# Windowed attention with a maxout feed-forward layer: a rewritten opening, masks added by TensorE, and Q in runs of four tokens

## The chip, the cores and the metric

The kernel runs on one core of a Trainium2 chip. The metric is the time of the program on the device in microseconds (us); a time given for a kernel is the median of several runs. A profile is one execution taken by the hardware profiler. Engines: PE is TensorE (matmul; PEld its weight loads), DVE is VectorE, ACT is ScalarE, POOL is GpSimd, SP is SyncE, which here only issues transfers. Each engine takes its instructions in the order of the program.

## What is computed

Four batches, eight heads, 768 tokens, head size 64. A query sees the first four tokens (the sink) and the 128 tokens up to itself. The result of attention, with the heads side by side, goes through a feed-forward layer that takes the maximum of three products.

```python
def _attn_ref(q, k, v, n_sink, window):            # n_sink 4, window 128
    scores = scale * np.matmul(q, k.transpose(0, 1, 3, 2))
    rel = pos[:, None] - pos[None, :]
    keep = (pos[None, :] < n_sink) | ((rel >= 0) & (rel < window))
    scores = np.where(keep, scores, -1000000000.0)
...
    return np.matmul(softmax(scores), v)           # softmax in words of numpy

x = attn_out.transpose(0, 2, 1, 3).reshape(B * S, H * D)     # 3072 x 512
h = np.maximum(np.maximum(x @ w1, x @ w2), x @ w3)           # 3072 x 768
return h @ w_out                                             # 3072 x 512, float32
```

## The kernel before

**Chunks.** The work is cut into 12 chunks of 256 tokens (three per batch; c is the chunk's place in its batch, and c = 0 has no chunk before it). A chunk has four pairs of heads p, each with two heads a. Each chunk goes through these steps, and all engines' orders are written out by hand; the framework adds the semaphores.

- `load` (L67): K, Q and V of the chunk, 0.5 MB each in float32, one transfer each on SP's queue. A partition holds a run of two tokens (i), 512 bytes, for each head. Two raw buffers per tensor.
- `cast` (L340, `cast_qk` L86, `cast_v` L95): to bf16, on POOL in the loop.
- `turn` (L100) or `turn_dma` (L113): K and Q are turned so that the head's 64 dimensions lie on partitions. `turn` uses eight PE transposes per tensor and copies (DVE for K, ACT for Q). `turn_dma` issues two transposing transfers of 64 partitions per tensor on SP (L117).
- `score` (L199): per pair two PSUM banks `st`, in which up to four blocks of 128 keys by 128 queries lie side by side (two half windows for each of two query halves). `sink_score` (L225): the four sink keys of all pairs in one bank, for c > 0.
- `expo` (L218): exp on ACT per head (L222), then one product with a 0/1 mask on DVE per pair (L223).
- `av_open`, `av` (L251, L266): values, with a column of ones that gives the sum; then reciprocal (L282) and product (L285) on DVE give `x_sb`.
- `xpose` (L290, PE and ACT) or `xpose_dma` (L299, one transposing transfer of 128 partitions on SP): x turned into `xT`.
- `ffn_h` (L307): eight matmuls for two of six blocks of the hidden layer and one of three weights; the first weight's result is copied by ACT (L320), the others are joined by a maximum on DVE (L322). Nine such groups per chunk.
- `ffn_y` (L326): six matmuls per half chunk, a copy by ACT (L333). `store` (L335): two transfers of 64 partitions on SP, since the queries lie in the order of Q's runs of two.

PSUM is one ring of eight banks (L55), so a matmul group waits until the group eight before it has been read.

**Opening (L350 to L433).** Chunk 0 goes through in two halves of its heads; POOL makes masks and the constants of the sink, then issues the weight transfers `load_w` (float32 to bf16, 0.75 MB written each) between its casts. Chunks 0, 1 and 2 are turned by PE, chunk 3 by SP.

**Loop (L435 to L476), i from 2.** A pass scores chunk n = i + 1, runs the hidden layer of chunk i and the output of chunk i - 1, and turns chunk i + 2. On SP its order is: loads of i + 3, turns of K and Q of i + 2, store of i - 1, turn of x of n.

Of the kernel before, what the change touches and what calls it, by code (L numbers as in the profile page):

```python
# [16 lines left out]
def kernel(  # L17
# [30 lines left out]

    with tc.manual_schedule():
# [7 lines left out]

        RING = 4
        kT = [const.tile([128, 2, NP, 2, 64], BF16, name=f"kT{i}") for i in range(RING)]
        qT = [const.tile([128, 2, NP, 2, 64], BF16, name=f"qT{i}") for i in range(RING)]  # L60
# [6 lines left out]
        def load(ci, what="kqv", eng=None, parts=1, gate=None):  # L67
            if ci >= NCH:
                return
            b, c = divmod(ci, CPB)  # L70
            t0 = c * 256
            for w in what:
                src = {"k": k, "q": q, "v": v}[w]
                if (ci, w) not in raws:
                    raws[ci, w] = raw.tile([128, H, 2, D], F32, tag=w + "_raw", name=w + "_raw")
                dst = raws[ci, w]
                if gate is not None:
                    gate.memset(dst[0:1, 0, 0, 0:1], 0.0)
                n = H // parts
                for g in range(parts):  # L80
                    (eng or nc.sync).dma_start(
                        out=dst[:, n * g:n * g + n],
                        in_=src[b, n * g:n * g + n, t0:t0 + 256]
                            .rearrange("h (p i) d -> p h (i d)", i=2))

        def cast_qk(ci, w, g, eng):  # L86

            if (ci, w) not in bfs:
                bfs[ci, w] = raw.tile([128, NP, 2, 2, D], BF16, tag=w + "_bf", name=w + "_bf")
            x, y = bfs[ci, w], raws[ci, w]  # L90
            eng.tensor_copy(  # L91
                x[:, 2 * g:2 * g + 2].rearrange("q p i a d -> q p a i d"),
                y[:, 4 * g:4 * g + 4].rearrange("q (p a) i d -> q p a i d", a=2))
# [6 lines left out]
        def turn(ci, w, g):  # L100

            pt = bank([128, 2, 2, 128], BF16, "pt")
            x = bfs[ci, w]
            for p in range(2):
                for i in range(2):
                    nc.tensor.transpose(  # L106
                        pt[:, p, i], x[:, 2 * g + p, i].rearrange("q a d -> q (a d)"), ident)
            dst = (kT if w == "k" else qT)[ci % RING]
            (nc.vector.tensor_copy if w == "k" else nc.scalar.copy)(
                dst[:, :, 2 * g:2 * g + 2].rearrange("q n p i r -> q n (p i) r"),  # L110
                pt.rearrange("q p i (n r) -> q n (p i) r", r=64))

        def turn_dma(ci, w):  # L113
            dst = (kT if w == "k" else qT)[ci % RING]
            x = bfs[ci, w].rearrange("q p i a d -> q (p i a d)")
            for n in range(2):
                nc.sync.dma_start_transpose(  # L117
                    out=dst[:, n].rearrange("q p i r -> q (p i) r"), in_=x[64 * n:64 * n + 64])

        load(0, "k", nc.sync, 2)  # L120
        load(0, "q", nc.scalar, 2)
        load(0, "v", nc.sync)
        load(1, "kqv", nc.sync)

        ident = const.tile([128, 128], BF16, name="ident")
        make_identity(nc, ident)
        sel = const.tile([128, 32], BF16, name="sel")


        msk = const.tile([128, 2, 4, 128], BF16, name="msk")  # L130
        msk0 = const.tile([128, 2, 3, 128], BF16, name="msk0")

        def masks():
            nc.gpsimd.memset(msk[:, 0, 0:2], 1.0)
            for i in range(2):
                hp = slice(64 * i, 64 * i + 64)
                nc.gpsimd.affine_select(
                    out=msk[hp, 0, 1], in_=msk[hp, 0, 1], compare_op=ALU.is_ge, fill=0.0,
                    base=-i, pattern=[[1, 2], [2, 64]], channel_multiplier=-2)
                nc.gpsimd.affine_select(  # L140
                    out=msk[hp, 0, 0], in_=msk[hp, 0, 0], compare_op=ALU.is_gt, fill=0.0,
                    base=i, pattern=[[-1, 2], [-2, 64]], channel_multiplier=2)
            nc.gpsimd.tensor_copy(msk0[:, 0, 0], msk[:, 0, 1])
            nc.gpsimd.tensor_copy(msk0[:, 0, 1], msk[:, 0, 0])
            nc.gpsimd.tensor_copy(msk0[:, 0, 2], msk[:, 0, 1])
            for i in range(2):
                nc.gpsimd.memset(msk0[64 * i:64 * i + 2, 0, 0:2], 1.0)
            nc.gpsimd.tensor_copy(msk0[:, 1], msk0[:, 0])

        def masks_late():  # L150
            nc.gpsimd.tensor_copy(msk[:, 0, 2:4], msk[:, 0, 0:2])
            nc.gpsimd.tensor_copy(msk[:, 1], msk[:, 0])

        bm = const.tile([128, 2], F32, name="bm")

        def sink_init():

            nc.gpsimd.memset(sel, 0.0)
            for a in range(2):
                nc.gpsimd.tensor_copy(  # L160
                    sel[:, 4 * a:4 * a + 4].rearrange("q (r i) -> q r i", i=2),
# [3 lines left out]

            nc.gpsimd.memset(bm, 0.0)
            for p in range(NP):
                nc.gpsimd.memset(bm[32 * p:32 * p + 8], 1.0)
                nc.gpsimd.affine_select(
                    out=bm[32 * p:32 * p + 8], in_=bm[32 * p:32 * p + 8], compare_op=ALU.is_ge,  # L170
                    fill=0.0, base=0, pattern=[[-4, 2]], channel_multiplier=1)
                nc.gpsimd.affine_select(
                    out=bm[32 * p:32 * p + 8], in_=bm[32 * p:32 * p + 8], compare_op=ALU.is_ge,
                    fill=0.0, base=3, pattern=[[4, 2]], channel_multiplier=-1)
# [9 lines left out]
        w_sb = []  # L184

        def load_w(wi):
            w = (moe_w1, moe_w2, moe_w3)[wi]
            wt = const.tile([128, DS, d_ff], BF16, name=f"w{wi}")
            nc.gpsimd.dma_start(out=wt, in_=w.rearrange("(a p) f -> p a f", p=128))
            w_sb.append(wt)  # L190
# [8 lines left out]
        def score(ci, pairs):  # L199
            b, c = divmod(ci, CPB)  # L200
            kc, qc = kT[ci % RING], qT[ci % RING]
            for p in pairs:
                st = [bank([128, 4, 128], F32, "st") for a in range(2)]
                for s, x, n, q0, q1 in ((0, kT[(ci - 1) % RING], 1, 0, 1), (1, kc, 0, 0, 2),
                                        (3, kc, 1, 1, 2)):
                    if s == 0 and c == 0:
                        continue
                    for a in range(2):
                        hp = slice(64 * a, 64 * a + 64)
                        nc.tensor.matmul(  # L210
                            st[a][:, s:s + q1 - q0],
                            lhsT=x[hp, n, p].rearrange("q i r -> q (i r)"),
                            rhs=qc[hp, q0:q1, p].rearrange("q n i r -> q n (i r)"),
                            start=True, stop=True)
# [3 lines left out]
        def expo(ci, p):  # L218
            lo = 0 if ci % CPB else 1
            e, st = es[ci, p]  # L220
            for a in range(2):
                nc.scalar.activation(e[:, a, lo:], st[a][:, lo:], AF.Exp, scale=scale)  # L222
            nc.vector.tensor_mul(e[:, :, lo:], e[:, :, lo:], msk0 if lo else msk)  # L223

        def sink_score(ci):  # L225
# [4 lines left out]
            for p in range(NP):  # L230
                nc.tensor.matmul(  # L231
                    st[32 * p:32 * p + 32], lhsT=ks[b % 2][:, p],
                    rhs=qT[ci % RING][:, :, p].rearrange("q n i r -> q n (i r)"),
                    start=True, stop=True, tile_position=(0, 32 * p))
            e = work.tile([128, 2, 128], BF16, tag="e_sink", bufs=2, name="e_sink")
            nc.scalar.activation(e, st, AF.Exp, scale=scale)  # L236
            es[ci, "sink"] = e

        def sink_v(b):
# [3 lines left out]
            for p in range(NP):  # L243
                nc.tensor.matmul(
                    sv[32 * p:32 * p + 32], lhsT=sel, rhs=x[:, 0, 2 * p:2 * p + 2],
                    start=True, stop=True, tile_position=(0, 32 * p))
            nc.vector.tensor_mul(vs[b % 2], sv, bm.unsqueeze(2).to_broadcast([128, 2, D + 1]))
# [87 lines left out]
        def store(ci, t0=0, t1=2):  # L335
            dst = out[ci * 256:ci * 256 + 256].rearrange("(t r i) d -> i r t d", t=2, i=2)
            for i in range(2):
                nc.sync.dma_start(out=dst[i, :, t0:t1], in_=ys[ci][64 * i:64 * i + 64, t0:t1])

        def cast(ci):  # L340
            if ci >= NCH:
                return
            for w in "kq":
                for g in range(2):
                    cast_qk(ci, w, g, nc.gpsimd)
# [4 lines left out]
        for x in vb:  # L350
            nc.vector.memset(x[:, :, :, D:D + 1], 1.0)
        masks()
        for g in range(2):
            for w in "kq":
                cast_qk(0, w, g, nc.vector)
                turn(0, w, g)
            score(0, range(2 * g, 2 * g + 2))
            for p in range(2 * g, 2 * g + 2):
                expo(0, p)
        for n in range(2):  # L360
            for i in range(2):
                cast_v(0, n, i, nc.gpsimd)
        load_w(0)
        load_w(1)
        sink_init()
        sink_k(0)
        masks_late()
        for g in range(2):
            cast_qk(1, "k", g, nc.vector)
            cast_qk(1, "q", g, nc.gpsimd)  # L370
        load_w(2)
        for n in range(2):
            for i in range(2):
                cast_v(1, n, i, nc.gpsimd)
        load_wo()
        av_open(0)
        for p in range(NP):
            av(0, p)
        xpose(0, 0)
        xpose(0, 1)  # L380
        for g in range(2):
            turn(1, "k", g)
            turn(1, "q", g)
        sink_v(0)
        sink_score(1)
        score(1, range(NP))
        expo(1, 0)
        expo(1, 1)
        load(2, gate=nc.vector)
        ffn_h(0, 0, 0)  # L390
        expo(1, 2)
        ffn_h(0, 1, 0)
        expo(1, 3)
# [124 lines left out]
```

## Time and profile before

| What | Value |
|---|---|
| Runs | 204.31, 205.11, 205.56 us; median 205.11 |
| Profiled execution | 206.73 us, span 205.0 us |
| PE matmuls of the hidden layer (L314) | 864, 107.1 us busy |
| exp (L222) | 96, 49.4 us busy; idle before 6.3 |
| mask product (L223) | 48, 34.2 us busy |
| maximum (L322) | 72, 49.2 us busy |
| casts on POOL (L91, L96) | 13.4 + 14.8 + 31.2 us busy |
| DMA queue of SP | 68992 packets, 31.73 MB |
| loads of K, Q, V | 0.5 MB each, 5.8, 6.6, 7.1 us from issue to landing |
| turn of K, Q, x by transfer | 4.4, 3.0, 3.3 us from issue to landing |
| weights | 7.2 us from issue to landing, `w_out` 9.1 |

The span runs from the first to the last instruction. A row of busy time is the sum over the instructions of one line. Matmuls are pipelined, so their busy time is longer than the spacing at which they are issued. A transfer's time is counted from its issue on the queue to the landing of its last byte. The granted clock is a share of TensorE's full speed.

### The profile page before, as it was taken

How to read it: one execution, taken by the hardware profiler on the slowest of the kernel's cores; microseconds unless marked ns; L12 is line 12 of the kernel's file. 1: busy time of each engine (PE TensorE's matmuls, PEld its weight loads, DVE VectorE, ACT ScalarE, POOL GpSimd, SP SyncE). 2: the span in 40 equal slices, each digit the busy share in tenths (PEclk: the TensorE clock that was granted, in tenths of full speed). 3: DMA queues.
4: the chain of work that ended last, by engine and by line, in shares of the span. 5: the costliest groups of instructions: out<-in, count | busy, mean ns of one | idle time of the engine just before them, and what ended most of it. 6: DMA issues, size and time to landing. Idle time of an engine off the chain costs nothing.

```text
span 205.0 us, 4504 instructions
## 1 busy us (share of the span) xinstructions
PE 174.1 (85%) x1788; PEld 129.8 (63%) x1800; DVE 111.5 (54%) x239; ACT 88.9 (43%) x177; POOL 71.9 (35%) x139
## 2 busy tenths in 40 slices
PE   0345978999739999999967999999999899999990
PEld 0223755896624976858735958858678488685860
DVE  1247263264831683864934845937739368286340
ACT  2412772225423537348163148264272661742321
POOL 7298702779204602611802706408227000000000
PEclk9999995799976999999997999999999999999999
DMA  5999999993569829979999989789899963142404
GB/s 153 290 200 204 184 161 290 294 276 105 132 109 299 167 52 252 176 176 295 96 137 294 181 218 243 165 207 244 146 268 167 173 110 99 35 102 51 106 0 102
DMA packets 72436, 35.68 MB, mean 174 GB/s; under 512 B 30176, under 2 KB 69344, under 8 KB 72416
## 3 DMA queue, kind: packets, MB, share of 16 engines
q1 hardware_dynamic: 68992, 31.73, 74.1%
q0 software_dynamic: 2368, 3.15, 9.9%
q10 hardware_dynamic: 1056, 0.52, 1.0%
q8 instruction: 14, 0.23, 0.5%
q14 instruction: 6, 0.05, 0.1%
HBM read 25.17 MB, written 6.29 MB: 153 GB/s over the span
## 4 chain that ended last, share of the span: by engine, by line
PE 48%; DMA 14%; ACT 11%; DVE 10%; issue 8%; SPq 4%; POOL 2%; DVEq 0%
PE h_ps L314 30%; PE y_ps L331 8%; ACT e_sb L222 7%; DMA xT<-x_sb 5%; DMA qT<-q_bf 4%; PE st L210 4%; DVE h_sb L322 3%; DMA q_raw<-in_q_dram 3%; DVE x_sb L285 3%; SPq L117 3%; PE pt L106 2%; PE o L277 2%; DMA k_raw<-in_k_dram 2%; ACT y_sb L333 2%; DVE e_sb L223 2%
## 5 line engine op out<-in xcount | busy, mean ns | idle before, releaser
L314 PE MATMUL h_ps<-xT,w 128*128 128x256 bf16 x864 | 107.1, 280 | 3.2 <-DMA xT<-x_sb 3.2
L314 PEld LDWEIGHTS <-w 128*128 128x128 bf16 x864 | 83.6, 100 | 17.4 <-DMA xT<-x_sb 5.0
L223 DVE TENSOR_TENSOR e_sb<-e_sb,msk 128x1024 bf16<-128x1024 bf16 (+1 forms) x48 | 34.2, 712 | 58.9 <-ACT e_sb L222 55.9
L322 DVE TENSOR_TENSOR h_sb<-h_sb,h_ps 128x512 bf16<-128x512 bf16 x72 | 49.2, 683 | 18.6 <-PE h_ps L314 16.4
L222 ACT ACTIVATE e_sb<-st 128x512 bf16<-128x512 f32 (+1 forms) x96 | 49.4, 585 | 6.3 <-PE st L210 6.3
L320 ACT CAST h_sb<-h_ps 128x512 bf16<-128x512 f32 x36 | 21.6, 601 | 47.8 <-PE h_ps L314 47.8
L91 POOL CAST k_bf<-k_raw 128x512 bf16<-128x512 f32 x20 | 13.4, 694 | 70.6 <-issue 42.0
L331 PE MATMUL y_ps<-wo,h_sb 128*128 128x512 bf16 x132 | 34.2, 392 | 1.1 <-DVE h_sb L322 0.2
L96 POOL CAST vb<-v_raw 64x512 bf16<-64x512 f32 x48 | 31.2, 650 | 10.6 <-DMA v_raw<-in_v_dram 8.6
L331 PEld LDWEIGHTS <-h_sb 128*128 128x128 bf16 x144 | 13.7, 100 | 17.9 <-issue 3.9
L333 ACT COPY y_sb<-y_ps 128x512 f32<-128x512 f32 x24 | 14.2, 592 | 21.8 <-PE y_ps L331 11.0
L285 DVE TENSOR_TENSOR x_sb<-o,rc 128x256 bf16<-128x256 f32 x48 | 20.4, 425 | 1.7
L277 PE MATMUL o<-vb,e_sb 128*128 128x65 bf16 x352 | 18.7, 197 | 1.7 <-DVE e_sb L223 1.7
L210 PE MATMUL st<-qT,kT 64*128 64x128 bf16 (+1 forms) x256 | 15.0, 256 | 4.7 <-DMA qT<-q_bf 2.3
L277 PEld LDWEIGHTS <-e_sb 128*128 128x128 bf16 x352 | 16.3, 100 | 4.1 <-DVE e_sb L223 2.2
L91 POOL CAST q_bf<-q_raw 128x512 bf16<-128x512 f32 x22 | 14.8, 699 | 3.6 <-DMA q_raw<-in_q_dram 3.4
L210 PEld LDWEIGHTS <-kT 64*128 64x128 bf16 x256 | 10.3, 101 | 8.4 <-issue 7.0
L106 PE MATMUL pt<-ident,k_bf 128*128 128x128 bf16 x24 | 3.3, 280 | 8.1 <-DVE k_bf L91 8.1
L296 PE MATMUL xt<-ident,x_sb 128*128 128x128 bf16 x24 | 4.3, 280 | 4.9 <-DVE x_sb L285 4.8
L282 DVE RECIPROCAL rc<-o 128x4 f32<-128x4 f32 x48 | 8.4, 175 | 0.1
L297 ACT COPY xT<-xt 128x512 bf16<-128x512 bf16 x6 | 3.2, 588 | 11.7 <-PE xt L296 11.7
L236 ACT ACTIVATE e_sink<-sk 128x256 bf16<-128x256 f32 x8 | 3.1, 384 | 11.6 <-PE sk L231 11.6
(46 smaller groups left out, 44.1 us busy)
## 6 DMA issues: line engine op xcount, KB each, us to landing
v_raw<-in_v_dram SPq DMA_DIRECT2D x12, 512.0 KB, 7.1
k_raw<-in_k_dram SPq DMA_DIRECT2D x11, 512.0 KB, 5.8
q_raw<-in_q_dram SPq DMA_DIRECT2D x11, 512.0 KB, 6.6
out_dram<-y_sb SPq DMA_DIRECT2D x22, 256.0 KB, 4.0
w<-in_moe_w_dram POOLq DMA_DIRECT2D x3, 768.0 KB, 7.2
wo<-in_moe_w_out_dram POOLq DMA_DIRECT2D x1, 768.0 KB, 9.1
q_raw<-in_q_dram ACTq DMA_DIRECT2D x2, 256.0 KB, 5.0
k_raw<-in_k_dram SPq DMA_DIRECT2D x2, 256.0 KB, 4.4
```

The costliest lines, as they stand in the source:

```text
L91: eng.tensor_copy(x[:, 2 * g:2 * g + 2].rearrange("q p i a d -> q p a i d"), y[:, 4 * g:4 * g + 4].rearrange("q (p a) i d -> q p a i d", a=2))
L96: eng.tensor_copy(vb[ci % RING][64 * i:64 * i + 64, n, :, 0:D], raws[ci, "v"][64 * n:64 * n + 64, :, i])
L210: nc.tensor.matmul(st[a][:, s:s + q1 - q0], lhsT=x[hp, n, p].rearrange("q i r -> q (i r)"), rhs=qc[hp, q0:q1, p].rearrange("q n i r -> q n ...
L222: nc.scalar.activation(e[:, a, lo:], st[a][:, lo:], AF.Exp, scale=scale)
L223: nc.vector.tensor_mul(e[:, :, lo:], e[:, :, lo:], msk0 if lo else msk)
L277: nc.tensor.matmul(o[:, t, a], lhsT=e[:, a, s], rhs=vb[cv % RING][:, n, 2 * p + a], start=first, stop=True, skip_group_check=True)
L285: nc.vector.tensor_mul(xs[ci][:, :, p], o[:, :, :, 0:D], rc.unsqueeze(3).to_broadcast([128, 2, 2, D]))
L314: nc.tensor.matmul(hp[:, f].rearrange("q (t r) -> q t r", t=2), lhsT=w_sb[wi][:, ds, c0:c0 + 128], rhs=xTs[ci][:, :, ds], start=(ds == 0), ...
L320: nc.scalar.copy(dst, hp)
L322: nc.vector.tensor_max(dst, dst, hp)
L331: nc.tensor.matmul(yp, lhsT=hs[ci][:, fb, t * 128:(t + 1) * 128], rhs=wo[:, fb], start=(fb == 0), stop=(fb == FB - 1))
L333: nc.scalar.copy(ys[ci][:, t], yp)
```

## The change

- **Q in runs of four.** A partition of `q_raw` holds four tokens of four heads (1024 bytes each); the lower 64 partitions take heads 0 to 3, the upper 64 heads 4 to 7, with one transfer for each. `turn_dma` turns Q in one transfer of 128 partitions. The scores' queries then lie as (i, r); exp writes them in natural order, every fourth element, so masks, values, x and the output are in natural order, and a store is one transfer of 128 partitions.
- **Masks added.** For chunks 0 and 1, PE first adds a mask of 0 or -2^30 to each bank (`ident` times `addm`), the scores accumulate on it, and the product on DVE is left out. The 0/1 masks for later chunks are worked out on POOL from `addm`.
- **Opening.** K of chunk 0 is cast by DVE and Q by ACT, all four halves before any score; V by DVE and POOL. Warm-up matmuls on zeros are added, 8 at the start and 6 before the first hidden group. The transfers of weights are issued earlier and in another order on POOL; loads of chunks 2 and 3 are released by POOL (after w1 has landed; after V of chunk 2 has been cast). Chunk 3 is turned by PE, its pass is written out, and the loop begins at i = 3.
- **Sink.** The selection is split by head, so that `sink_v` needs no mask.
- **Loop.** The load of i + 3 is written ahead of the cast of i + 2 (different engines); scores allocate two pairs' banks at a time.

```diff
-        def load(ci, what="kqv", eng=None, parts=1, gate=None):
+        def load(ci, what="kqv", gate=None, parts=1):
...
+                shape = [128, 2, 2, 4, D] if w == "q" else [128, H, 2, D]
+                dst = raws[ci, w] = raw.tile(shape, F32, tag=w + "_raw", name=w + "_raw")
                 if gate is not None:
-                    gate.memset(dst[0:1, 0, 0, 0:1], 0.0)
...
+                    gate(dst[0:1, 0, 0, 0, 0:1] if w == "q" else dst[0:1, 0, 0, 0:1])
+                if w == "q":
+                    for u in range(2):
+                        nc.sync.dma_start(
+                            out=dst[64 * u:64 * u + 64].rearrange("s w a i d -> s (w a) (i d)"),
+                            in_=src[b, 4 * u:4 * u + 4, t0:t0 + 256].rearrange(
+                                "h (s i) d -> s h (i d)", i=4))
...
         def turn_dma(ci, w):
...
+            if w == "q":
+                nc.sync.dma_start_transpose(
+                    out=qT[ci % RING].rearrange("q i w u n r -> q (i w) (u n r)"),
+                    in_=bfs[ci, w].rearrange("s i w a d -> s (i w a d)"))
+                return
...
         def masks_late():
...
+            for a in range(2):
+                nc.gpsimd.tensor_scalar(msk[:, a], addm, 2.0 ** -30, 1.0, op0=ALU.mult, op1=ALU.add)
...
-        def score(ci, pairs):
+        def score(ci, pairs, add=False):
...
+            if add:
+                m = addm if c else addm0
+                for p in pairs:
+                    for a in range(2):
+                        nc.tensor.matmul(
+                            sts[p][a][:, lo:].rearrange("q s (i r) -> q s i r", i=4),
+                            lhsT=ident, rhs=m.rearrange("q s (r i) -> q s i r", i=4),
+                            start=True, stop=False, skip_group_check=True)
...
-                            rhs=qc[hp, q0:q1, p].rearrange("q n i r -> q n (i r)"),
-                            start=True, stop=True)
+                            rhs=qc[hp, :, w, u, q0:q1].rearrange("q i n r -> q n i r"),
+                            start=not add, stop=True, skip_group_check=add)
...
-        def expo(ci, p):
+        def expo(ci, p, mul=True):
...
-                nc.scalar.activation(e[:, a, lo:], st[a][:, lo:], AF.Exp, scale=scale)
-            nc.vector.tensor_mul(e[:, :, lo:], e[:, :, lo:], msk0 if lo else msk)
+                nc.scalar.activation(
+                    e[:, a, lo:].rearrange("k s (r i) -> k s i r", i=4),
+                    st[a][:, lo:].rearrange("k s (i r) -> k s i r", i=4), AF.Exp, scale=scale)
+            if mul:
+                nc.vector.tensor_mul(e[:, :, lo:], e[:, :, lo:], msk0 if lo else msk)
...
         def store(ci, t0=0, t1=2):
-            dst = out[ci * 256:ci * 256 + 256].rearrange("(t r i) d -> i r t d", t=2, i=2)
-            for i in range(2):
-                nc.sync.dma_start(out=dst[i, :, t0:t1], in_=ys[ci][64 * i:64 * i + 64, t0:t1])
+            nc.sync.dma_start(
+                out=out[ci * 256:ci * 256 + 256].rearrange("(t p) d -> p t d", t=2)[:, t0:t1],
+                in_=ys[ci][:, t0:t1])
```

The new opening, in full but for the constants (`warm(n)` is n matmuls of 512 columns on zeros):

```python
load(0, "k", parts=2); load(0, "qv"); load(1)
...
warm(8); masks(); sink_init()
for g in range(2):
    cast_qk(0, "k", g, nc.vector); cast_qk(0, "q", g, nc.scalar)
for g in range(2): turn(0, "k", g)
for g in range(2): turn(0, "q", g)
score(0, (0, 2), add=True); score(0, (1, 3), add=True)
for p in (0, 2, 1, 3): expo(0, p, mul=False)
for i in range(2):
    cast_v(0, 0, i, nc.vector); cast_v(0, 1, i, nc.gpsimd)
load_w(0); sink_k(0)
for g in range(2): cast_qk(1, "k", g, nc.gpsimd)
load_w(1)
for g in range(2): cast_qk(1, "q", g, nc.scalar)
for g in range(2): turn(1, "q", g)
av_open(0)
for p in (0, 2, 1, 3): av(0, p)
for g in range(2): turn(1, "k", g)
xpose(0, 0); xpose(0, 1); sink_score(1)
score(1, (0, 2), add=True); score(1, (1, 3), add=True)
for i in range(2):
    cast_v(1, 0, i, nc.vector); cast_v(1, 1, i, nc.gpsimd)
load_w(2, 0, d_ff // 2); load_w(2, d_ff // 2, d_ff)
sink_v(0)
for p in (0, 2, 1, 3): expo(1, p, mul=False)
warm(6); ffn_h(0, 0, 0)
av_open(1); av(1, 0); av(1, 2); ffn_h(0, 1, 0); av(1, 1); ffn_h(0, 2, 0); av(1, 3)
masks_late()
load(2, gate=after_w1)        # POOL copies one element of w1 into each buffer
xpose(1, 0); xpose(1, 1)
cast_qk(2, "k", 0, nc.gpsimd); cast_qk(2, "k", 1, nc.gpsimd)
load_wo()
for fp in range(3): ffn_h(1, fp, 0)
for fp in range(3): ffn_h(0, fp, 1)
for fp in range(3): ffn_h(1, fp, 1)
cast_qk(2, "q", 0, nc.scalar); cast_qk(2, "q", 1, nc.scalar)
...
load(3, gate=pool_gate); load(4)      # POOL memset, after its casts of V of chunk 2
for fp in range(3): ffn_h(0, fp, 2)
for g in range(2): turn(2, "k", g); turn(2, "q", g)
ffn_h(1, 0, 2); sink_score(2); score(2, (0, 2)); score(2, (1, 3))
for p in (0, 2, 1, 3): expo(2, p)
ffn_h(1, 1, 2); ffn_h(1, 2, 2); ffn_y(0, 0)
av_open(2); av(2, 0); av(2, 2); ffn_y(0, 1); av(2, 1); av(2, 3)
store(0); cast(3, q=nc.scalar); xpose(2, 0); xpose(2, 1)
ffn_y(1, 0); ffn_y(1, 1); store(1)
for wi in range(3): ffn_h(2, 0, wi)
for g in range(2): turn(3, "k", g); turn(3, "q", g)
score(3, (0, 2)); score(3, (1, 3)); cast(4); turn_dma(4, "k"); turn_dma(4, "q")
...
for i in range(3, NCH):
...
    load(i + 3); cast(i + 2); turn_dma(i + 2, "k"); turn_dma(i + 2, "q")
```

## The prediction

> **What bounds the kernel now.** I read the page first, then the stage table, then the chain of waits with the timeline of the SP queue. The page says that TensorE is the busiest engine, and where it is not busy:
>
> ```profile
> PE 174.1 (85%) x1788; PEld 129.8 (63%) x1800; DVE 111.5 (54%) x239; ACT 88.9 (43%) x177; POOL 71.9 (35%) x139
> ...
> PE   0345978999739999999967999999999899999990
> ...
> PEclk9999995799976999999997999999999999999999
> DMA  5999999993569829979999989789899963142404
> ```
>
> Slices are 5.1 us. PE is idle or waiting before 20 us and around 55 us, and its granted clock falls in three places. The fourth row shows transfers nearly always in flight until 165 us. I cut the span at each pass of scores (c = 0 is a batch's first chunk):
>
> ```profile
> 0.00:32.70 32.70, 16.95 (x184) 11.94 (x185) 14.21 (x42) 14.01 (x28) 18.28 (x53) 0.98 1.05 203
> 32.70:60.60 27.90, 23.57 (x226) 17.92 (x225) 13.88 (x26) 10.24 (x20) 15.11 (x24) 0.87 0.83 198
> 60.60:74.94 14.34, 14.11 (x123) 10.25 (x124) 7.66 (x17) 6.02 (x13) 5.83 (x10) 0.83 0.83 183
> ...
> 88.50:102.80 14.30, 13.34 (x153) 10.10 (x153) 9.47 (x20) 7.08 (x14) 5.22 (x8) 1.00 1.01 194
> 102.80:119.10 16.30, 13.86 (x123) 10.37 (x124) 8.41 (x18) 6.03 (x13) 5.20 (x10) 0.90 1.05 207
> 119.10:132.30 13.20, 13.15 (x156) 10.09 (x156) 8.58 (x19) 7.08 (x14) 5.72 (x8) 1.00 1.05 209
> ...
> 158.90:173.60 14.70, 13.55 (x160) 10.18 (x160) 8.88 (x19) 7.19 (x14) 0.18 (x1) 1.00 0.68 126
> ```
>
> Columns: stretch, length, busy us of PE, PEld, DVE, ACT, POOL, granted clock, DMA share, GB/s. A loop pass that waits for nothing takes 13.2 us (12.9 where c = 0); the passes at 88.5, 102.8 and 158.9 take 1.1, 3.4 and 1.5 more. The first 74.94 us hold the hidden layer of three chunks, the attention of four and two outputs, what three free passes do in 39.6. What PE waits for, from the chain:
>
> ```profile
> 53.16 1.89 SPq L117
> 55.09 1.26 SPq L117
> 56.45 1.22 SPq L117
> 57.71 2.77 DMA qT<-q_bf
> ...
> 99.86 2.82 DMA qT<-q_bf
> 102.68 0.14 issue
> 102.81 0.24 PE st L210
> 103.06 5.67 DMA xT<-x_sb
> ```
>
> So after 50 us the chain runs through SP, which issues turns one after another, and through turns that land late. Before 33 us it runs through loads, casts, exp and x in series.
>
> **The change, part by part.**
>
> *Chunk 0.* K and Q (0.52 MB each) now start at 0.82 on SP alone; bytes flow from about 2.7 at 300 GB/s (0 to 10 us), so both Q halves are in at about 6.5. ACT casts (like its 0.59 copies), four transposes (0.61), copy (0.59): Q half g=0 is ready at 8.4. The mask adds are eight new matmuls of 384 columns: the output matmuls came every 0.43 us at half clock (62.8 to 65.4), so 0.32 each, the first four beside the copy. Scores 0.82 per eight. Second pair set: adds 1.3, scores 0.8, to 12.6; exps (0.82 a pair) end at 13.8. Before, they and the mask product end at 17.2. Gain 3.4, but part is spent: the Q casts of chunk 1 (1.2) now sit on ACT behind those exps, and PE reaches the value matmuls of chunk 0 only behind the transposes of that Q: 15.6, ending 17.3. x takes DVE 0.55 a pair, to 18.4 (before 20.1).
>
> *Chunk 1.* Transposes 0.9, K copies 0.9, then eight adds of 512 columns (0.22 to 0.43 each) and 24 score matmuls (1.1 to 1.4): second set ends 22 to 23.5. Exps (0.52 each, 4.1 + 0.4 sink) end at 25 to 26, without the 0.69 product behind each pair. Warm-up 6 x 0.22, three hidden groups of 0.88 and value groups of 0.25 fill PE to 28; x, transposes and two ACT copies (0.59 each) put the long hidden block at 30.7 instead of 32.7. Weights: the first w issue moves from 12.0 to about 9.5 (POOL, behind two V casts), data took 7 to 10 us to land, so w0 by 18 and w1 by 22, before use at 23 and 33. w2 (two issues) follows V of chunk 1, by 26; used at 39.
> *New gates.* POOL waits for w1 (about 22), then its copies let SP load chunk 2; queued behind on POOL are the K casts of chunk 2, the output weight's issue and V's casts. At 290 GB/s, beside w2 and wo (4 us each), K lands by 27, Q by 29, V by 31, wo (9.1 from issue to landing before) by 38; the transposes come at 41, wo's use at 46, so 8 us cover it, and nothing more is charged; without that cover POOL's 2.4 of casts and the landing would show, about 2. Chunk 3's loads wait on POOL for V's casts (34), chunk 4's on SP for the ACT cast of Q (36); used at 59 and 68. On SP, the turns of chunk 4 stand behind the store of chunk 1 (output copied at about 56): turns 56.6 to 60.4, landed by 64, 4 us early; the loads of chunk 5 stand behind them.
>
> *From the block to the loop pass that scores chunk 4* (74.94 before). Work: 24 hidden groups x 0.875 = 21.0, four outputs x 1.3 = 5.2, 32 transposes 1.8, scores 1.2 + 0.9, values 1.2 + 0.7, x transposes 0.7: 32.7. New waits: x of chunk 2 stands on DVE behind four mask products and two hidden maxima (0.69 each), so PE waits about 2.4 for it; after the transposes of chunk 3, PE waits about 1.0 for ACT's two copies. The PE turn of chunk 3 replaces the SP turn that held PE at 57 to 60.6. With 1.5 for the clock: 37.6, so 68.3. Gain 6.6.
>
> The clock term is bounded by rows. It fell at 31.6 after sparse work from 28.9 on, and returned at 38.0; after 2.5 idle us (106.3 to 108.8) it fell at 109.9 for 3.0 us, costing 1.5. The new gaps are 2.7 (before the block) and 2.4: cost 0 to 5.4, and I take one fall of 1.5. The Trainium skill (TensorE: Matmul & The Clock Gate, Why this matters for your kernels) allows idle gaps up to about 3 us; by it the term would be 0 and the sum 193.1, but the row with a fall after 2.5 us differs from it and decides.
>
> *The loop.* Per pass SP loses one of two Q turns (2.54 for two; x, of the same 128-row form, takes 1.26 for one) and one of two stores (1.28 for two): 1.9 less. One more Q load issue (0.6) stands ahead of the K turns, but these wait behind queued loads anyway (3.7 to 5.8 for two, where 2.5 is the least). At 102.8: Q lands 1.3 earlier, so PE's 0.9 wait goes; x was ready at 101.74 and issued at 103.06, so 1.3 of the 2.3 wait goes, perhaps the fall too; at the ninth pass x was ready at 158.25 and issued at 159.17, behind a store, so the 0.9 waited goes. Relief 0 (if landing, not issue, is late) to 6.0; by these, 1.1 (all of that pass's excess, the wait for Q) + 1.3 + 0.9 = 3.3. What is late next: x itself on DVE.
>
> Q's loads: 512 packets of 1 KB instead of 1024 of 512 B. If the packet count limits, 1.8 us per chunk becomes 0.9; but each load now fills 64 partitions, and stores from 64 partitions moved 206 GB/s (201 to 203 us) where loads moved 290, which gives 2.55. I take 1.8, no change; ends -0.9 and +0.75 per chunk. The Trainium skill (SBUF — State Buffer, Door 1: The DMA port swizzle) speaks against the change here: 64 partitions reach half the ports, 196 GB/s measured. By it Q's load would be 2.7, once 0.9 on the path, and the sum 195.5.
>
> *Exp writing every fourth element* has no row; the nearest is the contiguous exp, 0.52 for 512. Reading Q in runs of 32 by the score matmuls has none either (0.043 each now). I take no change for both; exp's end is twice its time (rival C), the matmuls' is 24 x 0.04 = 1 us a pass, and no end lies below nothing, since neither does less. The ACT casts of Q, POOL's four late mask products, four more sink matmuls per batch (0.06 each): off the path, under POOL's waits for loads.
>
> *End.* One last store instead of two: an issue of 0.6 less after the last copy. Gain 0.6 (to 1.2).
>
> Sum: 6.6 + 3.3 + 0.6 = 10.5. It is made on the span of 205.0; that execution's own time is 206.73, 1.7 around the span, and the median of runs is 205.11. I take the difference from the median: 194.6.
>
> **Rivals.** *A, the loop keeps its waits.* For: x landed 5.7 and 5.1 us after issue where 3.3 is the median, with the DMA share at 1.05; that is load, not issue. Against: fewer turns and packets. 205.1 - 7.2 = 197.9, 15%.
>
> *B, the opening gains little.* For: PE, in order, stands behind ACT's Q casts, behind DVE's x of chunks 1 and 2; two clock falls of 2.7 and w late by 2 would leave about 2 of 6.6. With the loop's relief partly kept: 201.5, 11%.
>
> *C, slower: exp's strided write.* Place: ACT, eight exps a pass, then product, then values. In the pass at 119.1 the last product ended at 127.65 and its values started at 129.39, 1.7 of slack. Price for d more per exp: 8 passes x (8d - 1.7) + 16d in the opening. It cancels the 10.5 at d = 0.30 (0.82 an exp); at twice (0.52 more) it is 28, giving 223. At d = 0.35: 209. Against: ACT's copies and casts, whatever their patterns, took 0.59 to 0.60 for 512. 11%.
>
> *D, more than forecast:* no fall, no gap at chunk 2, relief 6.0: 189, 9%.
>
> **How the numbers follow.** The forecast has 54%, alone 190.5 to 198.5. The range of 188.5 to 202.5 takes in A, B's middle and D, and leaves out C and B's tail, about 18%. A change of under 1% (2.05 us) can't be told from none. Faster: forecast, A, D and half of B, 0.84; same: B's rest, 0.05; slower: C, 0.11.
>
> **What would show it.** Right: the long hidden block starts near 30.7 and scores of chunk 4 near 68; exps of 512 in pairs at 1.1 us; one Q turn of about 1.3 in SP's queue per pass; no pass over 14 us. Wrong: exps over 0.8; hidden groups starting on a weight's landing; the clock at half for more than 5 us after 30; x turns landing after 5 us with PE waiting. If values of chunk 0 start after 17, the serial ACT order ate the gain.

## The result, and the profile after

The kernel after takes 248.49 us (247.18 to 250.28, four runs) beside 205.05 (204.31 to 205.56) before: a ratio of 1.213, with a 95% interval of 1.204 to 1.221. It is 43 us slower where 10.5 less was forecast. The profiled execution took 250.28 us, its span is 248.5.

From the page of the kernel after, the busy times and the 40 slices (6.2 us each here):

```profile
PE 199.2 (80%) x1849; PEld 139.7 (56%) x1862; DVE 107.7 (43%) x237; ACT 153.4 (62%) x187; POOL 62.6 (25%) x121
...
PE   7447967996798468888789897986997879879994
...
ACT  0595794349649448559549388298285693693311
...
PEclk9675988999799959799999997998899997997999
DMA  6999979940048769439539599099199560220212
```

ACT's busy time went from 88.9 to 153.4 us. The transfers, which were nearly always in flight before, now have slices at 0, and none of PE's listed waits names a transfer any more. The clock is below 9 in thirteen slices instead of five. The costliest groups on the page name the line, and the groups kept apart by shape (operation, shapes, count, busy us, mean ns of one, idle time before) say how much:

```profile
L261 ACT ACTIVATE e_sb<-st 128x512 bf16<-128x512 f32 x64 | 78.3, 1385 | 1.3 <-PE st L249 1.3
L261 ACT ACTIVATE e_sb<-st 128x384 bf16<-128x384 f32 x32 | 29.4, 1099 | 4.0 <-PE st L249 4.0
L280 ACT ACTIVATE e_sink<-sk 128x256 bf16<-128x256 f32 x8 | 6.0, 747 | 13.4 <-PE sk L274 13.4
```

The same groups before:

```profile
L222 ACT ACTIVATE e_sb<-st 128x512 bf16<-128x512 f32 x64 | 35.5, 627 | 0.2 <-PE st L210 0.2
...
L222 ACT ACTIVATE e_sb<-st 128x384 bf16<-128x384 f32 x32 | 13.9, 500 | 6.1 <-PE st L210 6.1
```

So the same 96 instructions on the same shapes take 107.7 us instead of 49.4. A duration of one overlaps with its neighbour's, so spacing is the better price: in the opening eight exps of 512 columns take 9.32 us, 1.17 each where they took 0.52, and eight of 384 take 6.99 (0.87, before about 0.42). How that reaches the end is read in the stages, cut at the scores of each chunk (columns as in the prediction's table; here the passes of chunks 4 and 5):

```profile
88.90:108.93 20.03, 17.54 (x155) 12.09 (x157) 8.10 (x18) 12.69 (x14) 5.13 (x8) 0.79 0.76 146
108.93:126.38 17.45, 14.16 (x151) 10.49 (x149) 7.79 (x17) 12.65 (x14) 5.07 (x8) 1.00 0.73 166
```

ACT is busy for 12.65 us of a pass that lasts 17.45, so it isn't simply full. The timeline of ACT and of PE in that pass shows how its order costs the rest (start, length, instruction, count, and in brackets the idle time before and what ended it):

```profile
109.05 0.74 ACT L280 ACTIVATE e_sink<-sk 128x256 bf16<-128x256 f32 x1 [1.40 <-PE sk L274]
109.54 2.53 ACT L261 ACTIVATE e_sb<-st 128x512 bf16<-128x512 f32 x2
...
118.49 2.48 ACT L261 ACTIVATE e_sb<-st 128x512 bf16<-128x512 f32 x2
120.94 0.59 ACT L366 CAST h_sb<-h_ps 128x512 bf16<-128x512 f32 x1
124.74 0.58 ACT L366 CAST h_sb<-h_ps 128x512 bf16<-128x512 f32 x1 [3.21 <-PE h_ps L360]
```

```profile
110.98 2.75 PE L377 MATMUL y_ps<-wo,h_sb 128*128 128x512 bf16 x11 [0.74 <-ACT e_sb L261]
113.57 2.94 PE L360 MATMUL h_ps<-xT,w 128*128 128x256 bf16 x24
...
117.10 0.21 PE L305 MATMUL o<-vs,e_sink 32*128 32x130 bf16 x1 [0.44 <-ACT e_sb L261]
118.24 0.21 PE L305 MATMUL o<-vs,e_sink 32*128 32x130 bf16 x1 [0.93 <-ACT e_sb L261]
```

From 109.05 to 121.5 ACT runs with one gap of 0.41, the copies of outputs and hidden groups among the exps. PE runs out of things it may do: the value banks (`av_open`, L305) take the places in PSUM that the scores hold until exp has read them. Then the exps are through, and ACT in its turn stands idle (3.21) while PE does the hidden groups. The two engines that ran side by side now wait for each other.

### The profile page after: what moved, and what is told of

It is laid out like the page before. It is cut to its first block, busy times and chain, and to the rows that moved or that the text cites. A ratio compares the mean times of both kernels' runs of the same rounds, so it can differ in the third digit from the quotient of the medians.

```text
span 248.5 us, 4603 instructions
## 1 busy us (share of the span) xinstructions
PE 199.2 (80%) x1849; PEld 139.7 (56%) x1862; DVE 107.7 (43%) x237; ACT 153.4 (62%) x187; POOL 62.6 (25%) x121
## 5 line engine op out<-in xcount | busy, mean ns | idle before, releaser
L360 PE MATMUL h_ps<-xT,w 128*128 128x256 bf16 x864 | 110.7, 284 | 9.0 <-ACT e_sb L261 6.6
L261 ACT ACTIVATE e_sb<-st 128x512 bf16<-128x512 f32 (+1 forms) x96 | 107.7, 1290 | 5.3 <-PE st L249 5.3
L360 PEld LDWEIGHTS <-w 128*128 128x128 bf16 x864 | 86.2, 102 | 26.3 <-issue 11.8
L265 DVE TENSOR_TENSOR e_sb<-e_sb,msk 128x1024 bf16<-128x1024 bf16 (+1 forms) x40 | 28.1, 702 | 83.5 <-ACT e_sb L261 83.5
L109 POOL CAST vb<-v_raw 64x512 bf16<-64x512 f32 x44 | 28.2, 642 | 17.6 <-DMA v_raw<-in_v_dram 16.0
L305 PE MATMUL o<-vs,e_sink 32*128 32x130 bf16 x64 | 7.4, 229 | 13.6 <-ACT e_sb L261 12.3
L280 ACT ACTIVATE e_sink<-sk 128x256 bf16<-128x256 f32 x8 | 6.0, 747 | 13.4 <-PE sk L274 13.4
L305 PEld LDWEIGHTS <-e_sink 32*128 32x128 bf16 x64 | 2.9, 92 | 18.4 <-issue 14.9
L103 POOL CAST q_bf<-q_raw 128x512 bf16<-128x512 f32 x16 | 9.8, 641 | 7.1 <-issue 3.5
L119 PE MATMUL pt<-ident,q_bf 128*128 128x128 bf16 x32 | 3.8, 263 | 9.1 <-ACT q_bf L103 9.1
```

The source lines that it names most:

```text
L109: eng.tensor_copy(vb[ci % RING][64 * i:64 * i + 64, n, :, 0:D], raws[ci, "v"][64 * n:64 * n + 64, :, i])
L261: nc.scalar.activation(e[:, a, lo:].rearrange("k s (r i) -> k s i r", i=4), st[a][:, lo:].rearrange("k s (i r) -> k s i r", i=4), AF.Exp, ...
L360: nc.tensor.matmul(hp[:, f].rearrange("q (t r) -> q t r", t=2), lhsT=w_sb[wi][:, ds, c0:c0 + 128], rhs=xTs[ci][:, :, ds], start=(ds == 0), ...
```

## Experiments

### Is it the write, and is there anything else?

The reordering of the queries can stand on either side of an exp: it writes in steps and reads PSUM without, as in the change, or it reads PSUM in steps and writes without gaps. The first run keeps all of the change but turns the two round:

```diff
-    e[:, a, lo:].rearrange("k s (r i) -> k s i r", i=4),
-    st[a][:, lo:].rearrange("k s (i r) -> k s i r", i=4), AF.Exp, scale=scale)
+    e[:, a, lo:].rearrange("k s (r i) -> k s r i", i=4),
+    st[a][:, lo:].rearrange("k s (i r) -> k s r i", i=4), AF.Exp, scale=scale)
```

(The same in `sink_score`.) 

> The kernel after, but exp reads its scores from PSUM in natural query order (every 32nd float32) and writes its result without gaps; nothing else is changed. Theory W (the loss is ACT's write of every fourth bf16 element): an exp of 512 takes 0.5 to 0.6 us again instead of 1.17 to 1.25, and the time falls to 192 to 202. Rival P (any pattern with gaps, on the read side too, slows ACT): exps stay above 1.0 and the time above 230. Rival O (the loss lies elsewhere, in the mask adds, the runs of 32 in the score matmuls or the new opening): exps at 0.5 to 0.6, time above 225.

It took 206.44 us (205.27 to 208.0; ratio 1.015, 1.009 to 1.021), above the 192 to 202 of theory W. The exps of 512 columns, kept apart by shape, are back where they were:

```profile
L261 ACT ACTIVATE e_sb<-st 128x512 bf16<-128x512 f32 x64 | 35.0, 623 | 2.6 <-PE st L249 2.4
```

Reading PSUM in steps of 32 floats (128 bytes) costs nothing here; writing every fourth bf16 costs 42 us. But the kernel is still no faster than before, so a second loss remains.

The second run leaves exp contiguous on both sides and lets the score matmuls, the sink's too, read Q in natural order, one element every 512 bytes (the mask matmuls then need no steps either):

```diff
-    rhs=qc[hp, :, w, u, q0:q1].rearrange("q i n r -> q n i r"),
+    rhs=qc[hp, :, w, u, q0:q1].rearrange("q i n r -> q n r i"),
```

> The kernel after, but the turn to natural order is made by the score matmuls: their moving operand is read with every query 512 bytes from the last, PSUM and exp are without gaps, and the mask adds read the mask without gaps. Theory W: exps at 0.5 to 0.6 us. The price goes to PE: the mask adds, whose moving operand lies 8 bytes apart, came every 0.49 us per 512 columns where the warm-up matmuls came every 0.25, so a score of 128 columns should go from 0.043 to 0.1 or more; 24 a pass are 1.4 us or more, and the time is 196 to 215. Mask adds at 0.22 to 0.25 each at full clock. Rival O: time above 225.

236.98 us (233.2 to 238.3; ratio 1.151, 1.130 to 1.171), above the 196 to 215 expected. The exps are short again (612 ns for 512 columns), and the price moves to PE:

```profile
L249 PE MATMUL st<-qT,kT 64*128 64x128 bf16 x160 | 27.5, 391 | 0.0
```

A score matmul of 128 columns takes 391 ns instead of 231, one of 256 takes 606 instead of 294. The matmuls behind them suffer too: in the pass whose scores start at 133.57, 24 scores take 3.65 us (1.06 in a free pass of the first run), and then eleven output matmuls take 4.45 instead of 2.76, at a granted clock of 0.59, although PE had no gap.

Two runs put nothing but the stepped write into the kernel before, with the scores still in Q's old order, so that masks and queries no longer belong together and the result is not the reference's:

```diff
-    nc.scalar.activation(e[:, a, lo:], st[a][:, lo:], AF.Exp, scale=scale)
+    nc.scalar.activation(
+        e[:, a, lo:].rearrange("k s (r i) -> k s i r", i=4),
+        st[a][:, lo:].rearrange("k s (i r) -> k s i r", i=4), AF.Exp, scale=scale)
```

> The kernel before, with exp writing every fourth element (64 bytes of each run of four queries at a time) and nothing else changed; the queries come out in another order within a block, so masks and rows no longer belong together. Theory W: an exp of 512 goes from 0.52 to 1.17 to 1.25 us; by the price in the prediction (8 passes x (8 x 0.7 - 1.7) + 16 x 0.7 in the opening = 42) 240 to 255. Rival O: below 215.

250.0 us (248.44 to 250.54; ratio 1.224, 1.213 to 1.235). The write alone, in the old kernel, costs as much as the whole change lost.

With `i=2`, every second element:

> The kernel before, with exp writing every second element (4 bytes apart) and nothing else changed; the queries come out in another order within a block. If leaving the run of neighbouring elements is what costs, an exp of 512 takes 1.1 to 1.3 us as with a step of four, and the time is as there; if the cost grows with the number of bytes passed over, 0.6 to 0.9 us and 208 to 228; if a step of two is free, 0.52 us and 205.

209.22 us (208.71 to 209.74, two runs; ratio 1.025, 1.011 to 1.040). The groups of exps of 512 columns in these two, every fourth element first, then every second:

```profile
L222 ACT ACTIVATE e_sb<-st 128x512 bf16<-128x512 f32 x64 | 78.5, 1373 | 0.1
```

```profile
L222 ACT ACTIVATE e_sb<-st 128x512 bf16<-128x512 f32 x64 | 43.6, 778 | 0.2 <-PE st L210 0.2
```

The cost is graded: 627 ns without gaps, 778 at every second element, 1373 at every fourth.

### The second loss: who holds the sink's keys

In the first run above the longest loop pass is that of chunk 4, 15.6 us behind a wait of 6.8; the passes after it take 13.1 to 14.2. PE's timeline there, and POOL's:

```profile
78.76 0.40 PE L274 MATMUL sk<-qT,ks 128*32 128x256 bf16 x4 [6.78 <-POOL ks L207]
79.09 1.89 PE L249 MATMUL st<-qT,kT 64*128 64x128 bf16 x24
...
81.74 3.64 PE L377 MATMUL y_ps<-wo,h_sb 128*128 128x512 bf16 x10 [0.22 <-issue]
```

```profile
72.03 1.17 POOL L105 CAST k_bf<-k_raw 128x512 bf16<-128x512 f32 x2 [14.56 <-PE sv L290]
74.20 1.18 POOL L103 CAST q_bf<-q_raw 128x512 bf16<-128x512 f32 x2 [1.00 <-DMA q_raw<-in_q_dram]
75.64 2.57 POOL L109 CAST vb<-v_raw 64x512 bf16<-64x512 f32 x4 [0.26 <-DMA v_raw<-in_v_dram]
78.27 0.44 POOL L207 COPY ks<-kT 64x16 bf16<-64x16 bf16 x2
```

PE waits 6.78 us for two copies of 64x16 elements. In POOL's order they stand behind all the casts of chunk 5. Those wait for its loads, and the first of these is issued on SP only at 66.82, behind the store of chunk 1 and the turns of chunk 4. After the gap PE's scores and outputs run at a granted clock of 0.50 (24 scores in 1.89 where a free pass takes 1.06). The keys that are copied had been ready since chunk 3 was turned. The kernel before has the copy at the same place, but there the loads of chunk 5 are issued at 59.03, and it runs at 70.49, ahead of its use at 75.01; the change wrote these loads behind the store of chunk 1. No run moves the loads back. Two runs write the copy ahead of the casts, one on top of the mended exp, one alone:

```diff
+            if not last and n % CPB == 1:
+                sink_k(n // CPB)
             load(i + 3)
             cast(i + 2)
...
                 if n % CPB == 1:
-                    sink_k(n // CPB)
                     sink_v(n // CPB)
```

> The kernel with exp reading in natural order and writing without gaps (206.4), and the sink's keys copied on POOL ahead of the casts of chunk i + 2 instead of behind them, in the passes that start a batch's second chunk. Theory S: the second loss is this copy, which stood on POOL behind the casts of chunk 5 and so behind loads that SP had not yet issued; PE waited 6.8 us for it in the pass of chunk 4 and ran about 3 us longer at half clock after it. Then no wait of sk for ks is over 0.5 us, the pass of chunk 4 takes 13 to 14 us, and the time is 194 to 199. Rival L: the late loads of chunk 5 come out in another wait (turns of K and Q, casts), and the time is 202 to 206.

199.11 us (197.83 to 200.97; ratio 0.975, 0.967 to 0.983), 7.3 less, just past theory S's upper end. No wait for `ks` is left. But the pass of chunk 4, which was to take 13 to 14, takes 16.5 us: its scores begin at 70.17 instead of 79.09, and PE now waits 0.5 us there for DVE to empty their banks, 1.2 for x to land, and 0.85 for DVE at the end of the pass.

> The kernel after, exp still writing every fourth element, with only the sink's keys copied ahead of the casts. If ACT's exps set the passes, the 4.3 us that PE waited for ks are worth little: 244 to 248.5. If the two losses simply add up, it is 238 to 241.

243.6 us (243.34 to 245.75; ratio 1.198, 1.188 to 1.207): 4.9 less than the kernel after, nearer to the first expectation and just past its end. The same edit is worth less beside a slow exp, where PE waits once for the keys (4.27 us), than without it, where it waits three times (8.6 in all): the slow exp hides part of the second loss.

### The opening: ACT's first instruction, and the masks

In the kernel after, ACT's timeline begins so:

```profile
7.81 1.28 ACT L103 ACT_TABLE_LOAD   x1 [7.81 <-DMA q_raw<-in_q_dram]
9.10 1.14 ACT L103 CAST q_bf<-q_raw 128x512 bf16<-128x512 f32 x2
```

And in the kernel before:

```profile
1.95 1.28 ACT L109 ACT_TABLE_LOAD   x1 [1.95 <-issue]
7.29 0.59 ACT L109 COPY qT<-pt 128x512 bf16<-128x512 bf16 x1 [4.06 <-PE pt L106]
```

The load of the function table belongs to ACT's first instruction with a function, in the kernel after the cast of Q, and there it starts only when the wait for Q's transfer is over. Before the change it ran at 1.95, 5.3 us ahead of the copy that it belongs to, although that copy waits for PE. So not every wait holds it back, and no run tells which ones do. One run adds a first instruction that waits for no transfer:

```diff
         nc.vector.memset(wz, 0.0)
+        nc.scalar.copy(wz[:, 0:1], wz[:, 1:2])
```

> The kernel with exp in order and the sink's copy first, and in addition a copy of one column of zeros on ACT as its first instruction, so that the table load (1.28 us) doesn't stand behind the wait for Q of chunk 0. Theory: Q's casts, exps of chunk 0, values and x all come 1.3 us earlier, and the time is 1.0 to 1.5 under that kernel's. Rival: PE's path through the opening is set elsewhere (V casts, K copies, weights), and it is within 0.4.

195.87 us (195.74 to 200.21; ratio 0.961, 0.954 to 0.968): 3.2 less, more than expected. In the traces 1.5 of it stands in the opening (scores of chunk 4 at 68.69 instead of 70.17) and 1.0 in the pass that follows, whose wait of 0.85 for DVE is gone; another 0.7 comes in the third pass of the loop, where the wait for Q's turn falls from 0.9 to 0.4. Why an earlier start removes these waits, no run tells.

The next run stores the added mask in the scores' order, so that its matmuls read without steps (POOL writes the mask so in the first place):

```diff
-    sts[p][a][:, lo:].rearrange("q s (i r) -> q s i r", i=4),
-    lhsT=ident, rhs=m.rearrange("q s (r i) -> q s i r", i=4),
+    sts[p][a][:, lo:],
+    lhsT=ident, rhs=m,
```

> The kernel with exp in order, the sink's copy first and the early table load, and the added masks stored in the scores' order of queries, so that the 16 mask matmuls read and write without steps. Theory: each takes 0.22 to 0.30 instead of 0.49 (0.17 to 0.25 instead of 0.38 for 384 columns), 1.6 us less per chunk on PE; the second banks of chunks 0 and 1 come about 1 us earlier each, and the time falls by 1 to 2 us. Rival: the masks run beside ACT's copies and exps, and the time moves by under 0.5.

194.40 us (194.14 to 194.6; ratio 0.954, 0.948 to 0.961): 1.5 less, as expected. The first four mask matmuls of 512 columns, in PE's timeline of the kernel with steps (the run before this one) and of the one without, both at a granted clock of 1.00:

```profile
20.18 1.97 PE L237 MATMUL st<-addm,ident 128*128 128x512 bf16 x4
```

```profile
19.78 1.04 PE L243 MATMUL st<-addm,ident 128*128 128x512 bf16 x4
```

Four take 1.97 or 1.04 us. With steps they took the same 1.97 in the first run, at a granted clock of 0.50: the clock makes no difference to them. The smaller ones, at a clock near 0.5 in both kernels, hardly gain (1.54 against 1.48 for the first four). In the traces the opening gains 2.8 (scores of chunk 4 at 65.90 instead of 68.69), and the pass behind it gives 1.2 back (16.7 against 15.5).

### Is the loop's relief what the prediction said?

Four runs change one thing each in that last kernel, all on one chip, where the kernel before took 205.0 (201.32 to 206.67). That last kernel itself ran on another chip, so the ratios to the kernel before are what can be compared. First the store, again in two transfers:

```diff
-    nc.sync.dma_start(out=out[...].rearrange("(t p) d -> p t d", t=2)[:, t0:t1], in_=ys[ci][:, t0:t1])
+    dst = out[...].rearrange("(t p) d -> p t d", t=2)
+    for i in range(2):
+        hp = slice(64 * i, 64 * i + 64)
+        nc.sync.dma_start(out=dst[hp, t0:t1], in_=ys[ci][hp, t0:t1])
```

> The kernel with exp in order, the sink's copy first, the early table load and the masks in the scores' order (194.4), with each store again issued as two transfers of 64 partitions, as in the kernel before. By the prediction's terms for one store (0.9 in the passes where x's turn stands behind a store, 0.6 at the end) it takes 0.6 to 1.5 more: 195 to 195.9. Rival: SP no longer sets a pass, and only the end moves: 194.2 to 195.

200.68 us: five of six runs between 200.24 and 201.64, one 196.62, so neither expectation. The profiled execution is one of the five (201.64). It loses most of its time in two passes, of 15.4 and 17.5 us, where Q's and x's turns land late, and in the second PE's clock falls to 0.55 behind a wait of 2.49 us for x. The same instructions also ran in 196.62, so the difference can't be read as the price of a second store, and that price stays open.

Next Q, again turned by two transfers of 64 partitions:

```diff
-    nc.sync.dma_start_transpose(
-        out=qT[ci % RING].rearrange("q i w u n r -> q (i w) (u n r)"),
-        in_=bfs[ci, w].rearrange("s i w a d -> s (i w a d)"))
+    for u in range(2):
+        nc.sync.dma_start_transpose(
+            out=qT[ci % RING][:, :, :, u].rearrange("q i w n r -> q (i w) (n r)"),
+            in_=bfs[ci, w][64 * u:64 * u + 64].rearrange("s i w a d -> s (i w a d)"))
```

> The same kernel (194.4) with Q again turned by two transfers of 64 partitions, so that SP has one more transposing transfer in each pass. By the prediction's terms for one Q turn (1.1 in the pass that waits for Q, 1.3 or more where x's turn is issued late) it takes 1.1 to 3.5 more: 195.5 to 197.9. Rival: the turns of K and Q wait for their landing anyway, and the time is within 0.5: 193.9 to 194.9.

196.03 us (194.52 to 197.66; ratio 0.969, 0.959 to 0.979). It lies on the prediction's side, but its interval overlaps that of the kernel with one turn (0.948 to 0.961), so the Q turn's part isn't settled.

Without both groups of warm-up matmuls:

> The same kernel (194.4) without the 8 and the 6 warm-up matmuls, which feed nothing. Theory: they hold the granted clock up through the opening; without them the hidden groups of chunk 0 run at half clock and the time grows by 1 to 3: 195.4 to 197.4. Rival: the clock follows the real work, and the 6 before the first hidden group (1.4 on the chain) only stand in the way: 193 to 194.2.

193.67 us (192.05 to 195.16; ratio 0.955, 0.945 to 0.965), not to be told from the kernel with them. The first four slices of the granted clock read 9996 without and 9966 with them, but the first four mask matmuls take 1.49 us without and 1.48 with them, so nothing in chunk 0 runs faster for them, whatever the clock's record says (the lines stand with the next run). The long hidden block begins at 29.59 instead of 30.51. Where they stand, they don't hold the clock up.

Last, Q of chunk 0 loaded on ACT's queue beside K on SP's, which is where the kernel before loads it (there in two transfers of 128 partitions):

```diff
-        load(0, "qv")
+        load(0, "q", qeng=nc.scalar)
+        load(0, "v")
```

> The same kernel (194.4) with the two loads of Q of chunk 0 issued on ACT's queue, beside K on SP's. Theory: Q landed at 7.8 instead of the predicted 6.5 because its two halves (64 partitions each) were issued behind K and one after the other; side by side with K they land at 6.3 to 7.0, and the time falls by 0.8 to 1.5: 192.9 to 193.6. Rival: the bytes of K and Q together set the landing, Q stays at 7.5 to 8, and the time is within 0.4.

194.26 us (192.81 to 197.44; ratio 0.958, 0.948 to 0.968), and ACT's cast of Q starts at 8.11 instead of 7.79: as the rival says, issue order doesn't set the landing. With Q on SP, the transfers move 138 to 240 GB/s in slices of 0.2 us between 4.1 and 7.3 us, while Q's halves are carried, but for three slices of 282 to 328; before, with 128 partitions, they stay at 287 or more. That points to the 64 partitions, but no run changes them alone.

The time is no clean measure of this, since something else moved. The warm-up matmuls wait for ACT's first copy, which now stands behind Q's two issues, so they begin at 3.72 instead of 2.29. The first mask matmuls with the warm-up as it was, without it, and with it later:

```profile
9.32 1.48 PE L243 MATMUL st<-addm,ident 128*128 128x384 bf16 x4
```

```profile
9.44 1.49 PE L243 MATMUL st<-addm,ident 128*128 128x384 bf16 x4
```

```profile
9.54 0.81 PE L244 MATMUL st<-addm,ident 128*128 128x384 bf16 x4
```

With the later warm-up PE waits 0.62 us for Q instead of 2.17, the granted clock is 1.00 from 9 to 11 us instead of 0.52, and the masks take 0.81. In this one trace, then, warm-up matmuls that end shortly before the work did go with a full clock in it.

| Kernel | Median us | Ratio to before |
|---|---|---|
| after | 248.49 | 1.213 |
| + exp written without gaps | 206.44 | 1.015 |
| + sink's keys ahead of the casts | 199.11 | 0.975 |
| + early table load | 195.87 | 0.961 |
| + masks in the scores' order | 194.40 | 0.954 |

The last row beats both kernels, 4.6% under before (3.9 to 5.2%).

## Why the prediction was wrong

**The step that failed** is "I take no change for both", where "both" are exp writing every fourth element and the scores reading Q in runs of 32. For the write it failed. The other half held: 24 score matmuls that read Q in runs of 32 take 1.06 us in the first run, as in a free pass before. Rival C put the mechanism in the right place: ACT, eight exps a pass, the point of decision at d = 0.30. Its end of "twice its time" was too near: spacing grew by 0.65 at 512 columns and 0.45 at 384. The rival's own formula, with these, gives 6 x (8 x 0.65 - 1.7) + 2 x (8 x 0.45 - 1.7) = 24.8 in the loop and 8 x 0.65 + 8 x 0.45 = 8.8 in the opening: 33.6 (its first factors are the loop passes of 512 and of 384 columns), where undoing the write gave 42.1. Between the traces with and without it, the opening up to the scores of chunk 3 differs by 10.5 (75.22 against 64.70), near the formula. From the scores of chunk 4 on it is 33.1 (159.6 against 126.5): passes of 512 columns lose 4 or more, not 3.5, since PE and ACT also wait for each other in turn, and in three of those passes the clock fell (0.79, 0.91, 0.91). The argument for it, that ACT's copies and casts took 0.59 to 0.60 "whatever their patterns", rested on rows none of which wrote single elements in steps: in the kernel before, ACT's copies and casts write runs of 256 elements or more. The Trainium skill (SBUF — State Buffer, Door 1: The DMA port swizzle, in its note on cachelines) says that a stride of up to 8 bf16 elements is free. The runs differ for ACT's writes: 1.24 times the duration at 2 elements, 2.2 times at 4.

**A queue not followed.** The prediction listed POOL's gates and SP's order ("the loads of chunk 5 stand behind them"), but not that the sink's keys for chunk 4 were behind the casts of chunk 5 on POOL, and so behind those loads. It was worth 7.3 once exp was mended. The copy's place was old; what was new was the late issue of the loads. All links but one were in the text; the missing one was two instructions of 0.2 us.

**The opening's terms.** Q of chunk 0 was to be in at 6.5 and came at 7.8, and between 7.6 and 8.9 in the mended kernels. Here the choice of "1.8, no change" for Q's load failed, and the rule that the prediction set against it (Door 1, 2.7 by 64 partitions) was the nearer: by it Q lands at 7.4. The masks were to take 0.32 and 0.22 to 0.43; they took 0.38 and 0.49, with steps of 8 bytes in what PE reads. The table load (1.28) behind Q's wait wasn't in the sum. Without it, in the kernel with three mends (exp, sink, table), the long hidden block still begins at 32.8 instead of 30.7; with the masks' steps gone too it begins at 30.5. The clock fall of 1.5 that was charged didn't come: in the kernel with three mends the gaps before the block are 0.57 and 0.94, not 2.7, and the clock is 1.00 from 31.64 on. (The row that charged it, a gap of "2.5 idle us", stands in the profile's waits as 2.31.) So errors of both signs met, and that the scores of chunk 4 begin at 68.69, where 68.3 was forecast, is partly luck.

**The loop.** In that kernel the rest after 68.69 takes 125.4, before it took 130.1 after 74.94: a relief of 4.7 with the end, where 3.3 + 0.6 was forecast; up to 1.7 of it may belong to the profiled execution of the kernel before, which took 206.73 beside a median of 205.05. That kernel still carries the strided masks, so it is the change as the prediction pictured it, with three faults removed, and it takes 195.87 beside 194.6; as a ratio 0.961 (0.954 to 0.968) where 0.949 was forecast. Most of the gain was there; it was first lost to exp, and then to the late loads behind which POOL's copy stood. What each of the store and the turn gives stays open: the runs with two of each don't settle it.

"If values of chunk 0 start after 17, the serial ACT order ate the gain": in the kernel after they start at 21.1, with the mended exp at 18.9, with the early table and contiguous masks at 16.1. "Exps over 0.8" was the sign that mattered, and the first one to look at.

## What to carry to other kernels

When a change moves a permutation into an instruction that had none, choose the side where the step is free: here reading PSUM in steps by ACT cost nothing, while ACT's write or PE's read in steps of four elements cost about twice the time. A price without a row, multiplied by 96 instructions on an engine that others wait for, is worth a bound well past "twice", and the bound should set the forecast unless a row excludes it. Follow each tiny copy through its engine's order: on an in-order engine it inherits every wait of the transfers ahead of it.

## What was not expected of the hardware

- ACT writing bf16 in steps: 512 columns in 627 ns (mean of one) without gaps, 778 at every second element, 1373 at every fourth; its read of PSUM at every 32nd float, 623.
- PE reading its moving operand in steps of 8 bytes: 512 columns every 0.49 us, at a granted clock of 1.00 and of 0.50 alike, and 0.26 without steps at 1.00; in steps of 512 bytes 391 ns for 128 columns, against 231 in runs of 32. Behind 3.65 us of such reads, without a gap, the granted clock was 0.59.
- ACT's table load (1.28 us) stood behind the wait for a transfer of the first instruction that needs it (at 7.81), and ahead of a wait for PE in another kernel (at 1.95).
- In the loops of the kernels with the mended exp, the clock fell after idle gaps of PE of 6.8 and 2.5 us, and not after gaps of 2.2 or less. A long gap isn't needed where work is sparse: in the kernel after, PE was busy for 0.64 us between 98 and 100, with no gap over 0.92, and the clock was 0.50 between 102 and 104.
